# Sliding-window attention beside a squared-ReLU FFN: scores of later blocks in four 64x64 quarters, with a raw exp tile, other load and split orders, and wide dummy matmuls

## The chip, the cores and the metric

One core of a Trainium2 chip runs the whole program. The metric is the device time of one execution in microseconds (us); a figure for a kernel is the median of its runs. The profile is one further execution, recorded by the hardware profiler; its times count from the start of the first recorded instruction (the span).

## What is computed

The shapes are batch 8, heads 8, sequence 576, head width 64; the FFN has 4608 tokens (8 x 576), model width 512 and hidden width 2048. Results are float32.

```python
scores = scale * np.matmul(q, k.transpose(0, 1, 3, 2))
rel = pos[:, None] - pos[None, :]
bias = slopes[:, None, None] * (-np.abs(rel).astype(np.float32))[None, :, :]
mask = (rel >= 0) & (rel < window)            # window = 128
scores = np.where(mask, scores + bias[None], -1000000000.0)
attn = softmax(scores)                        # over keys
x = (attn @ v), heads side by side            # 4608 x 512
h = x @ w_in;  r = np.maximum(h, 0.0);  g = r * r
out = g @ w_out
```

A query sees itself and the 127 keys before it. With blocks of 128 queries and keys, a query block needs its own key block (where the key is not after the query) and the one before it (where the key's place in its block is greater than the query's place in its own). In each of these two 128x128 squares one 64x64 quarter is empty: in the own square, keys 64 to 127 for queries 0 to 63; in the square of the earlier block, keys 0 to 63 for queries 64 to 127.

## The kernel before

**Blocks.** Each batch's 576 positions make five blocks (`NKB`), four of 128 and one of 64; block m is number m % 5 (kb) of batch m // 5, 40 in all. The last block of a batch and the first of the next are scored together as a pair, in one P tile.

**Stages of a block.** `load_block` loads k, q and v, cast to bf16, through POOL's queue (block 0's k and q through SP's, in float32). `turn` transposes k and q: on TensorE for the blocks in `KQ_PE` (with evacuations to kqT on ScalarE and VectorE), otherwise by a DMA from SP's queue. `layout` places the score parts in the P tile: for a full block the earlier keys at columns 128 to 255 of each head, the own keys at 0 to 127. `score` takes units of half a block (4 heads) and makes one burst on TensorE of two units at the start and three from block 5 on. For each of a unit's two head pairs c and for each part there are two matmuls, one for each half of the array's 64 rows (heads on partitions 0 to 63 and 64 to 127 of kqT), which write two PSUM banks. Then for each bank an exp on ScalarE (L536) writes P from PSUM, and a multiplication on VectorE (L543) applies the mask with its ALiBi decay, in place. `mix` multiplies P by V with a column of ones beside it (L564), takes reciprocals of the sums (L587), normalizes into x (L592), and transposes x into xT on TensorE for blocks in `X_PE` (L610), otherwise by a DMA from SP's queue (L602).

**FFN.** Tokens go in nine groups of 512. `fc_step` computes a hidden slice with w_in (L667: 4 matmuls per 128 hidden columns), ReLU on ScalarE (L676), the square on VectorE into g (L683). `t_part` multiplies g by w_out (L729: 16 matmuls per 128 tokens), followed by an evacuation and a store. The first two groups are cut into pieces of tokens (`SPLIT`), so that they can start before all of the group's x is there.

**What sets the order.** Every step is a `Task` with assumed costs per engine, a key (its due time; `where` gives it for attention, with `AHEAD` and `LEAD` moving it forward), dependences, and slots that it takes and frees. `Plan.order` runs through these with a list scheduler and fixes the order of each engine; the program is then written out in that order, and engines only wait for semaphores. All PSUM slots are one pool of eight banks, and a score burst takes two for each unit. The ring sizes are in `size`. `FIRST` writes out the order of the first loads (b a block, i a quarter of w_in, o a quarter of w_out). `warm` at the start and `filler` in planned idle times of TensorE issue matmuls on zeros: `WARM` of them at the start, and afterwards `FILL` of the planned idle time until `UNTIL`; before `COLD` the plan counts TensorE at half speed. `QUARTERS` is set in this kernel but not used.

## Time and profile before

| quantity | value |
|---|---|
| median of 14 runs | 311.47 us (310.77 to 313.35) |
| profiled execution, its own time | 312.18 us |
| span of the profile | 310.4 us |
| TensorE matmul busy | 304.5 us (98%) |
| ScalarE busy | 179.1 us (58%) |
| VectorE busy | 161.2 us (52%) |
| exp L536, 128x512 | 124 instructions, 609 ns mean |
| mask L543, 128x512, single blocks | 96 instructions, 421 ns mean |
| score matmuls L507 | 576 |
| granted TensorE clock | 1.00 |

How to read the profile: busy time of TensorE overlaps from one matmul to the next, so differences between the starts of consecutive matmuls say what each costs in a stream. "PE" is TensorE's matmuls, "PEld" its weight loads, "DVE" VectorE, "ACT" ScalarE, "POOL" GpSimd, which here issues the loads, and "SP" the engine that issues stores and transposing DMAs. A row of groups gives the line, the engine, the operation, the tiles written and read, their shape, the count, busy us and mean ns. A row of waits gives the engine and line that waited, for what, the us in total, the number of times and the longest. A row for a stretch gives its length and, for PE, PEld, DVE, ACT and POOL in this order, busy us and the number of instructions, then the granted clock, the DMA share and GB/s. Time between engines matters only where TensorE waits for it.

### The profile page before, as it was taken

Reading aid. Unit: us, or ns where it says so; the run is one execution under the profiler, and the core shown is the slowest. Engines: PE = TensorE matmul, PEld = TensorE weight load, DVE = VectorE, ACT = ScalarE, POOL = GpSimd, SP = SyncE. Lnnn points to the kernel's source line nnn. Section 1 sums busy time; section 2 is a strip of 40 time slices with the busy share of each in tenths; the row PEclk is TensorE's granted clock in tenths of the full one; section 3 lists DMA queues with packets and bytes.
Section 4 is the critical chain, followed back from the end, with each engine's and each line's share of the span. In section 5 each row is a group of like instructions: output and inputs, shape, how many; then the busy total and the mean of one; then the engine's idle time right before and its main releaser. Section 6 shows DMA issues by size and latency. Waiting matters only on the chain.

```text
span 310.4 us, 7396 instructions
## 1 busy us (share of the span) xinstructions
PE 304.5 (98%) x2945; PEld 177.6 (57%) x2945; DVE 161.2 (52%) x475; ACT 179.1 (58%) x336; POOL 107.4 (35%) x134
## 2 busy tenths in 40 slices
...
GB/s 130 174 189 181 183 173 123 129 148 133 137 150 153 143 156 154 130 155 165 214 103 207 143 225 201 123 127 186 76 88 84 54 59 34 36 35 34 34 97 74
DMA packets 168115, 39.88 MB, mean 128 GB/s; under 512 B 159440, under 2 KB 163792, under 8 KB 168080
## 3 DMA queue, kind: packets, MB, share of 16 engines
...
q8 instruction: 23, 0.38, 0.5%
q14 instruction: 12, 0.10, 0.1%
...
## 4 chain that ended last, share of the span: by engine, by line
PE 93%; DMA 3%; POOL 2%; DVE 1%; ACT 0%; issue 0%; POOLq 0%
PE A L667 41%; PE A L729 40%; PE A L564 5%; PE A L507 5%; DMA kq<-in_q_dram 3%; PE A L458 1%; POOL kq L388 1%; PE A L610 1%; POOL vt L388 1%; ACT kqT L407 0%; DVE kqT L405 0%; POOL w_in_sb L357 0%; POOL dist L274 0%; DVE xT L405 0%; DVE g L683 0%
## 5 line engine op out<-in xcount | busy, mean ns | idle before, releaser
L667 PE MATMUL A<-xT,w_in_sb 128*128 128x512 bf16 (+3 forms) x960 | 150.6, 294 | 0.0
L729 PE MATMUL A<-w_out_sb,g 128*128 128x512 bf16 (+2 forms) x592 | 147.8, 373 | 0.0
L676 ACT ACTIVATE rt<-A 128x512 bf16<-128x512 f32 (+1 forms) x146 | 85.4, 600 | 73.1 <-PE A L667 62.9
L683 DVE TENSOR_TENSOR g<-rt 128x512 bf16<-128x512 bf16 (+1 forms) x146 | 60.9, 418 | 84.6 <-ACT rt L676 83.7
L667 PEld LDWEIGHTS <-w_in_sb 128*128 128x128 bf16 x960 | 71.0, 98 | 47.6
L729 PEld LDWEIGHTS <-g 128*128 128x128 bf16 x592 | 54.6, 98 | 56.5
L536 ACT ACTIVATE P<-A 128x512 bf16<-128x512 f32 (+1 forms) x132 | 68.4, 595 | 18.3 <-PE A L507 18.3
L543 DVE TENSOR_TENSOR P<-P,masks 128x512 bf16<-128x512 bf16 (+1 forms) x104 | 42.3, 411 | 19.9 <-ACT P L536 16.3
L388 POOL DMA_DIRECT2D vt<-in_v_dram x40 | 33.9, 850 | 52.6 <-PE A L564 39.9
L388 POOL DMA_DIRECT2D kq<-in_k_dram x39 | 33.2, 852 | 35.3 <-DMA kqT<-kq 21.6
L388 POOL DMA_DIRECT2D kq<-in_q_dram x39 | 33.4, 856 | 13.2 <-DMA kq<-in_k_dram 4.9
L699 ACT ACTIVATE osb<-A 128x512 f32<-128x512 f32 (+1 forms) x36 | 21.7, 602 | 22.2 <-PE A L729 22.0
L564 PEld LDWEIGHTS <-P 128*128 128x128 bf16 x576 | 26.3, 98 | 12.7
L592 DVE TENSOR_TENSOR x<-A,rec 128x256 bf16<-128x256 f32 (+1 forms) x80 | 32.3, 415 | 0.6
L707 POOL DMA_DIRECT2D out_dram<-osb x3 | 1.7, 563 | 80.3 <-ACT osb L699 80.3
L564 PE MATMUL A<-vt,P 128*128 128x65 bf16 x576 | 29.2, 193 | 0.0
L507 PEld LDWEIGHTS <-kqT 64*128 64x128 bf16 x576 | 15.0, 94 | 8.4 <-issue 7.6
L587 DVE RECIPROCAL rec<-A 128x4 f32<-128x4 f32 (+1 forms) x80 | 13.6, 177 | 8.9 <-PE A L564 7.7
L507 PE MATMUL A<-kqT,kqT 64*128 64x128 bf16 (+1 forms) x256 | 16.8, 211 | 0.7 <-ACT kqT L407 0.3
L507 PE MATMUL A<-kqT 64*128 64x128 bf16 (+1 forms) x320 | 17.3, 211 | 0.0
L543 DVE TENSOR_TENSOR P<-P,pair_masks 128x512 bf16<-128x512 bf16 x28 | 11.6, 419 | 3.4 <-ACT P L536 2.6
L407 ACT ACTIVATE kqT<-A 128x512 bf16<-128x512 bf16 (+1 forms) x9 | 5.2, 580 | 8.7 <-DVE kqT L405 5.9
...
## 6 DMA issues: line engine op xcount, KB each, us to landing
...
```

Of the source, the lines that this page charges most:

```text
L388: nc.gpsimd.dma_start(o, src[b, :, kb * 128:kb * 128 + n, :].rearrange("h s d -> s h d"))
L507: nc.tensor.matmul(slots[ms[0], 2 * j + half].tile.rearrange("p (c x) -> p c x", c=2)[:, c % 2, at:at + w], kqT[sk_of[mk].idx][rows, c, :] ...
L536: nc.scalar.activation(Pv(i), view(slot.tile.rearrange("p (c x) -> p c x", c=2)), AF.Exp, bias=0.0, scale=scale)
L543: nc.vector.tensor_tensor(pt, pt, view(mk), op=ALU.mult)
L564: nc.tensor.matmul(bank(slot_v)[:, hi * (D + 1):(hi + 1) * (D + 1)], Pt[sP.idx][:, place(h)].rearrange("p t q -> p (t q)")[:, at_of[m, par ...
L587: nc.vector.reciprocal(srec.tile[0:n, :], pv[0:n, :, D])
L592: nc.vector.tensor_tensor(xt[sx.idx][0:n, hf * 256:(hf + 1) * 256].rearrange("p (h e) -> p h e", h=4), pv[0:n, :, 0:D], srec.tile[0:n, :]. ...
L667: nc.tensor.matmul(bank(slot)[:, fi * w:(fi + 1) * w], w_in_sb[:, cc, fc * 128:(fc + 1) * 128], xT[:, cc, g * 512 + lo:g * 512 + hi], star ...
L676: nc.scalar.activation(srt.tile[:, 0:cols], slot.tile[:, 0:cols], AF.Relu, bias=0.0, scale=1.0)
L683: nc.vector.tensor_tensor(sg.tile[:, fcs[0]:fcs[-1] + 1, lo:hi], r, r, op=ALU.mult)
L699: nc.scalar.activation(so.tile[:, lo:hi], slot.tile[:, lo:hi], AF.Copy)
L729: nc.tensor.matmul(bank(slot)[:, lo:hi], sg.tile[:, fc, t * 128:(t + 1) * 128], w_out_sb[:, fc, lo:hi], start=fc == 0, stop=fc == FCB - 1)
```

## The change

**Scores.** With `QUARTERS = 6`, every block from number 6 on that is neither paired nor the first of a batch (kb 1, 2 or 3) is scored in quarters. For each head pair c the two 128x128 parts become four pieces: own keys 0 to 63 with queries 0 to 127, own keys 64 to 127 with queries 64 to 127, earlier keys 64 to 127 with queries 0 to 127, earlier keys 0 to 63 with queries 0 to 63. Each is a matmul per row half, with a 64x64 stationary operand, writing partitions 0 to 63 or 64 to 127 of the bank: eight matmuls per head pair instead of four. The columns of the upper keys are moved left by 64, so a head has 192 packed columns on every partition.

**Exps and masks.** The exp of such a bank reads 2 x 192 columns and writes a tile of a new ring `raw` (2 tiles). Two multiplications on VectorE, one per key half, take it to its place in a tile of another new ring `Pq` (2 tiles), columns 0 to 191 for keys 0 to 63 and 64 to 255 for keys 64 to 127. The quarters that are never written are set to zero once, by four memsets at the start. P is taken by the first mask rather than by the burst. The P-times-V matmuls stay as they are; the first of each half waits for the masks of its half.

**Constants.** `FIRST` loads blocks 0 to 3 before w_in. The first group is split in two pieces of 256 tokens (before: four of 128), the second in three (before: four). `X_PE` gains blocks 6, 13 and 21, `KQ_PE` loses block 11. `AHEAD`, `LEAD` and `EARLY` shift due times; `SOON` and the plan's cost of an exp (50 ns more) change what the planner assumes. The kq ring has 8 tiles instead of 7.

**Dummies.** A dummy matmul now streams up to 512 columns of zeros (four times the same 128) instead of 128; `WARM` is 24 x 128 columns instead of 16, `FILL` 0.7 instead of 0.8, `COLD` 8.2 us instead of 5.

The shortcut in `Plan.order` (left out below) skips candidates that can't be the best, and the field `n` of a task is not read.

```diff
--- before.py
+++ after.py
...
@@ -210,20 +213,20 @@
     NG = NT // 512
     NBLK = B * NKB
 
-    FIRST = "b0 b1 i0 b2 i1 b3 i2 o0 b4 i3 b5 o1 b6 o2 b7 o3 b8 b9"
-    SPLIT = {0: [(0, 128), (128, 256), (256, 384), (384, 512)], 1: [(0, 192), (192, 320), (320, 448), (448, 512)]}
-    EARLY = -20
-    AHEAD = {10: -60, 1: 30, 4: 30, 9: -60, 5: 0, 0: 0, 12: 60, 11: 0, 2: 60, 8: 30, 7: 60, 6: 0, 3: 30, 24: -30, 14: -60, 18: 30, 25: 30, 23: 30, 16: -30, 13: 60, 21: 0, 19: 30, 17: 0, 22: 0}
-    LEAD = 20
-
-    KQ_PE = [0, 1, 2, 3, 4, 5, 6, 7, 8, 11]
-    X_PE = [0, 1, 2, 3, 4, 5, 7, 8, 12, 17]
-    WARM = 16
-    FILL, UNTIL = 0.8, 26e3
-    COLD = 5000
-    QUARTERS = 99
+    FIRST = "b0 b1 b2 b3 i0 i1 i2 b4 b5 o0 b6 o1 b7 o2 i3 o3 b8 b9"
+    SPLIT = {0: [(0, 256), (256, 512)], 1: [(0, 192), (192, 320), (320, 512)]}
+    EARLY = 0
+    AHEAD = {10: -30, 1: 30, 4: 90, 9: -60, 5: 30, 0: 0, 12: 60, 11: 0, 2: -60, 8: 0, 7: 90, 6: 0, 3: -30, 24: 0, 14: -30, 18: 30, 25: 30, 23: 30, 16: -30, 13: 30, 21: 0, 19: 30, 17: 0, 22: 0, 20: 60, 15: 30}
+    LEAD = 40
+
+    KQ_PE = [0, 1, 2, 3, 4, 5, 6, 7, 8]
+    X_PE = [0, 1, 2, 3, 4, 5, 6, 7, 8, 12, 13, 17, 21]
+    WARM = 24
+    FILL, UNTIL = 0.7, 26e3
+    COLD = 8200
+    QUARTERS = 6
     V0 = 1
-    SHARE, SOON = 3, 500
+    SHARE, SOON = 3, 1500
     LONG, UNITS = 5, 3
     W_IN = [0, 4, 8, 12, 16]
     PAIR_AFTER, PAIR_KEY = 1, -140
...
@@ -250,11 +253,12 @@
         return [const.tile(shape, BF16, name=f"{name}_{i}") for i in range(n)]
 
 
-    size = {"kq": 7, "v": 7, "kqT": 5, "P": 2, "x": 4}
+    size = {"kq": 8, "v": 7, "kqT": 5, "P": 2, "x": 4, "Pq": 2, "raw": 2}
     kq = ring("kq", size["kq"], [128, 2, d_model])
     vt = ring("vt", size["v"], [128, H, D + 1])
     kqT = ring("kqT", size["kqT"], [128, 2 * C, 128])
-    Pt = ring("P", size["P"], [128, H, 2, 128])
+    Pt = {nm: ring(nm, size[nm], [128, H, 2, 128]) for nm in ("P", "Pq")}
+    raw = ring("raw", size["raw"], [128, H, 192])
     xt = ring("x", size["x"], [128, d_model])
 
     plan = Plan({"rec": 4, "rt": 3, "g": 2, "osb": OSB, **size}, BANKS, COLD, (SHARE, SOON))
...
@@ -338,11 +342,16 @@
     zero_first("v", vt, lambda t: t[64:128, :, 0:D], 512)
     zero_first("kq", kq, lambda t: t[64:128], 512)
     zero_first("kqT", kqT, lambda t: t[:, 0:C, 64:128], 128)
+    t_zero_P = []
+    for t in Pt["Pq"]:
+        t_zero_P.append(zero_task(t[0:64, :, 1, 64:128], 512))
+        t_zero_P.append(zero_task(t[64:128, :, 0, 0:64], 512))
+
     def warm():
-        for i in range(WARM):
-            nc.tensor.matmul(bank(sw)[:, 0:128], zero, zero, start=True, stop=True)
+        idle(bank(sw), WARM)
     sw = Slot("A")
-    plan.add({"PE": 53.5 * WARM}, -9.1e5, warm, [t_ones], [sw], [sw]).cols = 128 * WARM
+    tw = plan.add({"PE": 53.5 * WARM}, -9.1e5, warm, [t_ones], [sw], [sw])
+    tw.cols, tw.n = 128 * WARM, -(-WARM // 4)
 
     def load(key, ns, emit, deps=(), acq=()):
         return plan.add({"POOL": 900.0}, key, emit, deps, acq, dma=ns)
...
@@ -472,8 +481,9 @@
 
 
     def layout(ms):
-        sP = Slot("P")
         pair = len(ms) == 2
+        quarters = not pair and ms[0] % NKB and blk[ms[0] % NKB] == 128 and ms[0] >= QUARTERS
+        sP = Slot("Pq" if quarters else "P")
         work_of = []
         for i, m in enumerate(ms):
             b, kb, n, _, first = where(m)
@@ -500,7 +510,18 @@
             for sl in slots.values():
                 bank(sl)
             for (ms, sP, work_of, _), j in units:
-                for c in (2 * j, 2 * j + 1):
+                for c in (2 * j, 2 * j + 1) if sP.tag == "Pq" else ():
+                    m = ms[0]
+                    for part, k0, q0, q1 in ((1, 0, 0, 128), (1, 64, 64, 128), (0, 64, 0, 128), (0, 0, 0, 64)):
+                        mk = m - 1 + part
+                        lo = (c % 2) * 256 + at_of[m, part] + q0 - k0
+                        for half in range(2):
+                            rows = slice(half * 64, half * 64 + 64)
+                            nc.tensor.matmul(
+                                slots[m, 2 * j + half].tile[k0:k0 + 64, lo:lo + q1 - q0],
+                                kqT[sk_of[mk].idx][rows, c, k0:k0 + 64], kqT[sk_of[m].idx][rows, C + c, q0:q1],
+                                start=True, stop=True)
+                for c in () if sP.tag == "Pq" else (2 * j, 2 * j + 1):
                     for m, mk, w, at, _ in work_of:
                         for half in range(2):
                             rows = slice(half * 64, half * 64 + 64)
@@ -508,10 +529,13 @@
                                 slots[ms[0], 2 * j + half].tile.rearrange("p (c x) -> p c x", c=2)[:, c % 2, at:at + w],
                                 kqT[sk_of[mk].idx][rows, c, :], kqT[sk_of[m].idx][rows, C + c, 0:w],
                                 start=True, stop=True)
-        tm = plan.add({"PE": 220.0 + 2 * sum(max(w[2], 64) / 2.4 + 4 for u in units for w in u[0][2])}, due - 28, burst,
+        cost = 220.0 + 2 * sum(88.0 if u[0][1].tag == "Pq" else sum(max(w[2], 64) / 2.4 + 4 for w in u[0][2])
+                               for u in units)
+        tm = plan.add({"PE": cost}, due - 28, burst,
                       [t for u in units for w in u[0][2] for x in w[:2] for t in t_kq_of[x]] + chain["s"],
-                      [*slots.values()] + [u[0][1] for u in first_of],
+                      [*slots.values()] + [u[0][1] for u in first_of if u[0][1].tag == "P"],
                       [x for u in units if u[1] == 1 for w in u[0][2] for x in w[4]])
+        tm.n = 4 * sum(4 if u[0][1].tag == "Pq" else len(u[0][2]) for u in units)
         plan.bursts.append(tm)
         chain["s"] = [tm]
         for (ms, sP, work_of, due), j in units:
@@ -526,16 +550,37 @@
                     return t
                 return t.rearrange("p c (t q) -> p c t q", t=2)[:, :, lo:hi, 0:n]
 
-            for i in (2 * j, 2 * j + 1):
+            for i in (2 * j, 2 * j + 1) if sP.tag == "Pq" else ():
                 slot = slots[ms[0], i]
+                if i == 0:
+                    raw_of[ms[0]] = Slot("raw")
+                sr = raw_of[ms[0]]
+
+                def expo(i=i, slot=slot, sr=sr):
+                    nc.scalar.activation(raw[sr.idx][:, 2 * i:2 * i + 2],
+                                         slot.tile.rearrange("p (c x) -> p c x", c=2)[:, :, 0:192],
+                                         AF.Exp, bias=0.0, scale=scale)
+                te = plan.add({"ACT": act(384) + 50.0}, due - 28 + 3 * i, expo, [tm], [sr] if i == 0 else [], [slot])
+                for k0 in (0, 64):
+                    def mask(i=i, k0=k0, sr=sr, sP=sP):
+                        nc.vector.tensor_tensor(
+                            Pt["Pq"][sP.idx].rearrange("p h t q -> p h (t q)")[k0:k0 + 64, 2 * i:2 * i + 2, k0:k0 + 192],
+                            raw[sr.idx][k0:k0 + 64, 2 * i:2 * i + 2],
+                            masks.rearrange("p h t q -> p h (t q)")[k0:k0 + 64, 2 * i:2 * i + 2, k0:k0 + 192],
+                            op=ALU.mult)
+                    P_of[ms[0]][1].append(plan.add(
+                        {"DVE": dve(384, 2)}, due - 28 + 3 * i, mask, [te] + t_zero_P + t_mask,
+                        [sP] if i == 0 and k0 == 0 else [], [sr] if i == 3 and k0 else []))
+            for i in () if sP.tag == "Pq" else (2 * j, 2 * j + 1):
+                slot = slots[ms[0], i]
 
                 def Pv(i=i, sP=sP, view=view):
-                    return view(Pt[sP.idx][:, 2 * i:2 * i + 2].rearrange("p h t q -> p h (t q)"))
+                    return view(Pt["P"][sP.idx][:, 2 * i:2 * i + 2].rearrange("p h t q -> p h (t q)"))
 
                 def expo(i=i, Pv=Pv, view=view, slot=slot):
                     nc.scalar.activation(Pv(i), view(slot.tile.rearrange("p (c x) -> p c x", c=2)),
                                          AF.Exp, bias=0.0, scale=scale)
-                te = plan.add({"ACT": act(cols)}, due - 28 + 3 * i, expo, [tm], [], [slot])
+                te = plan.add({"ACT": act(cols) + 50.0}, due - 28 + 3 * i, expo, [tm], [], [slot])
 
                 def mask(i=i, pair=pair, Pv=Pv, view=view):
                     pt = Pv(i)
@@ -563,7 +608,7 @@
                     def emit(h=h, hi=hi, part=part, mk=mk, slot_v=slot_v):
                         nc.tensor.matmul(
                             bank(slot_v)[:, hi * (D + 1):(hi + 1) * (D + 1)],
-                            Pt[sP.idx][:, place(h)].rearrange("p t q -> p (t q)")[
+                            Pt[sP.tag][sP.idx][:, place(h)].rearrange("p t q -> p (t q)")[
                                 :, at_of[m, part]:at_of[m, part] + 128],
                             vt[s_in[mk, "v"].idx][:, h, :],
                             start=part == p0, stop=part == 1)
...
@@ -575,8 +620,8 @@
                             rel.append(sP)
                     new = hi == 0 and part == p0
                     last = plan.add({"PE": mm(D + 1)}, due - 12 + 4 * hf, emit,
-                                    [last, t_P[place(h) // 2], t_in[mk, "v"]]
-                                    + (t_P[2 * hf:2 * hf + 2] + chain["pv"] if new else []),
+                                    [last, t_in[mk, "v"]]
+                                    + (t_P[len(t_P) // 2 * hf:len(t_P) // 2 * (hf + 1)] + chain["pv"] if new else []),
                                     ([slot_v] + ([sx] if hf == 0 else [])) if new else [], rel)
             chain["pv"] = [last]
             srec = Slot("rec")
...
@@ -763,15 +809,18 @@
             t_part(g, u // 4, u % 4, key)
             key += 4
 
+    def idle(tile_, n):
+        for i in range(0, n, 4):
+            w = min(4, n - i)
+            nc.tensor.matmul(tile_[:, 0:128 * w].rearrange("p (w x) -> p w x", w=w), zero,
+                             zero.unsqueeze(1).to_broadcast([128, w, 128]), start=True, stop=True)
+
     def filler(slot, n):
         def emit():
-            for i in range(n):
-                if slot.turns:
-                    nc.tensor.transpose(bank(slot)[:, 0:128], zero, ident)
-                else:
-                    nc.tensor.matmul(bank(slot)[:, 0:128], zero, zero, start=True, stop=True)
-        t = Task({"PE": 107.0 * n / 2}, 0, emit, [t_ones] + [t_ident16] * slot.turns, [slot])
-        t.eng, t.start, t.end, t.seq, t.cols = "PE", 0.0, 0.0, 0, 128 * n
+            bank(slot)
+            idle(banks[slot.tag][slot.idx], n)
+        t = Task({"PE": 53.5 * n}, 0, emit, [t_ones], [slot])
+        t.eng, t.start, t.end, t.seq, t.cols, t.n = "PE", 0.0, 0.0, 0, 128 * n, -(-n // 4)
         return t
 
     def fill(tasks):
```

## Prediction

> **What bounds the kernel now.** I first read the busy shares and the chain that ended last, on the page.
>
> ```profile
> PE 304.5 (98%) x2945; PEld 177.6 (57%) x2945; DVE 161.2 (52%) x475; ACT 179.1 (58%) x336; POOL 107.4 (35%) x134
> ...
> PE 93%; DMA 3%; POOL 2%; DVE 1%; ACT 0%; issue 0%; POOLq 0%
> PE A L667 41%; PE A L729 40%; PE A L564 5%; PE A L507 5%; DMA kq<-in_q_dram 3%; PE A L458 1%; POOL kq L388 1%; PE A L610 1%; POOL vt L388 1%; ACT kqT L407 0%; DVE kqT L405 0%; POOL w_in_sb L357 0%; POOL dist L274 0%; DVE xT L405 0%; DVE g L683 0%
> ```
>
> The end is set by TensorE from start to finish. Busy time says little there, because matmuls overlap (a 512-column one lasts 379 ns, but the next starts 216 ns after it). So I take start-to-start times from the trace, which add up without overlap: the two FFN products (L667, L729) 252.0 us, probabilities times V (L564) 18.0, scores (L507) 17.1, transposes (L458, L440, L610) 7.9, dummy matmuls (L343, L770, L772) 11.3; sum 306.3. The first matmul starts at 1.0 us and 3.1 us follow the start of the last, which gives the span of 310.4. Only work in this list, and waits put into it, can move the time.
>
> Next, who TensorE waits for, and where the dummies lie (the four stretches are start-up, filling, attention beside FFN, FFN alone; the second answer counts the dummies only).
>
> ```profile
> PE A L458 <- DMA kq<-in_k_dram: 1.2, 1, 1.2
> PE A L343 <- DVE vt L322: 1.0, 1, 1.0
> PE A L507 <- ACT kqT L407: 0.3, 1, 0.3
> PE A L507 <- DVE kqT L405: 0.2, 1, 0.2
> ```
>
> ```profile
> 50.00:247.00 197.00, 197.00 (x1932) 108.33 (x1930) 117.37 (x345) 126.22 (x237) 71.07 (x86) 1.00 1.42 144
> ```
>
> ```profile
> 0.00:22.90 22.90, 11.40 (x121) 9.53 (x121) 0.11 (x1) 1.00 1.53 164
> ```
>
> All waiting lies in the first 23 us. From 50 to 247 us TensorE has no idle time and a full granted clock, VectorE is busy 117.4 of 197 us (60%) and ScalarE 126.2 (64%).
>
> **The score matmuls.** A quarter-packed block is any of kb 1 to 3 from block 6 on: 3 in each of 7 batches, 21 blocks, 84 head pairs. The cost of a head pair is read in the timeline of one burst.
>
> ```profile
> 103.63 0.38 PE L729 MATMUL A<-w_out_sb,g 128*128 128x512 bf16 x1
> 103.94 0.23 PE L507 MATMUL A<-kqT,kqT 64*128 64x128 bf16 x2
> 104.01 0.22 PE L507 MATMUL A<-kqT 64*128 64x128 bf16 x2
> 104.06 0.22 PE L507 MATMUL A<-kqT,kqT 64*128 64x128 bf16 x2
> 104.12 0.22 PE L507 MATMUL A<-kqT 64*128 64x128 bf16 x2
> ...
> 104.56 0.22 PE L507 MATMUL A<-kqT 64*128 64x128 bf16 x2
> 104.72 0.39 PE L667 MATMUL A<-xT,w_in_sb 128*128 128x512 bf16 x1
> ```
>
> Each "x2" is the two row halves of the array working side by side, 3 to 4 ns apart, and such a pair takes 56 ns: 53 for 128 columns plus the 3 ns step. A head pair has two of them, 112 ns. In the burst at 63.8 us, pairs with 64 columns start 25 to 29 ns apart although each brings two weight loads, so columns set the pace and an instruction costs next to nothing.
>
> The change makes eight 64x64 matmuls of this head pair: pairs A (128 columns, lower keys), B (64, upper), C (128, upper), D (64, lower). Nothing in this trace writes half of the output partitions, so the cost is bounded.
> *Low end:* upper and lower keys run side by side too. A and B start together; C follows B after 27 ns and ends at about 87; D follows A at 56 and ends at 83. The next head pair starts at about 86: 26 ns saved, times 84, is 2.2 us.
> *High end:* they take turns: 56+29+56+29 = 170 ns, 58 more, times 84, is 4.9 us lost.
> *Between:* weight loads. The Trainium skill speaks against the change here: "TensorEngine Tiling (Array Packing)", section Feature Incompatibilities, says that column tiling and Fast Weight Load exclude each other, and "TensorE: Matmul & The Clock Gate", section LDWEIGHTS, gives a plain load as columns / 1.2 ns, an estimate of 53 ns for 64 columns. The nearest rows are these.
>
> ```profile
> L440 PEld LDWEIGHTS A<-ident,kq 128*128 128x128 f32 x8 | 1.2, 185 | 0.0
> L458 PEld LDWEIGHTS <-kq 128*128 128x128 bf16 x72 | 4.4, 98 | 2.1 <-DMA kq<-in_k_dram 1.4 <-DMA kq<-in_q_dram 0.3
> ```
>
> A load of 4-byte weights lasts 87 ns longer than one of bf16, which fits slow loads of about that price. If the two key halves load side by side but slowly, C waits for its weights until 57 ns, D until 61, the next A until 114: 114 ns against 112, a loss of 0.2 us over 84. By the row of fast bf16 loads it is 86 ns.
> I take 86 ns, -2.2 us: a 64-column load is half the size of those now hidden inside 25 to 29 ns, and the four tiles use separate weights. The rule keeps a case of its own.
>
> Changing the array's split costs time: 312 ns from the start of the last 512-column matmul to the burst against 216, and as much on leaving (148 after the second of a pair against 53), 96 ns each way. Eight of the bursts from 50 us on hold units of both kinds (those with 64-column pair units among 128-column ones), so each gains one switch inside: 8 x 0.096 = +0.8 us; zero if the switch between two 64-row splits is free.
>
> **Exps and masks.** An exp goes from 512 to 384 columns: 84 x (609 - 500) = 9 us less on ScalarE (531 and 490 ns are the rows at 128x384). A mask of 421 ns becomes two on 64 partitions each; 64x256 and 128x256 normalizations take 408 and 416 ns, so half the partitions do not halve it, and the row at 384 columns is 348 ns: 168 x 348 - 84 x 421 = +23 us on VectorE. Both count nothing on the path as long as TensorE keeps FFN matmuls to run: VectorE goes to (117.4+23)/197 = 71%. A burst's masks take 12 x 348 = 4.2 us instead of 2.5; behind them on VectorE queue the squares of L683, which feed L729, and the reciprocals of L587. The new waits (an exp for its raw buffer, freed by the last mask two blocks earlier; a first mask for P) sit on ScalarE and VectorE, while the burst itself no longer waits for P. If this cover is gone, each of the 14 bursts with quarters would show up to 1.7 us. I take 0. Four memsets of 485 ns join VectorE's start-up (14.9 of 22.9 us busy): 0 to +0.5, taken 0.
>
> **Start-up.** Loads arrive in one queue in issue order. In the trace v of blocks 0 and 1 is in at 9.4 us, the first w_in quarter at 13.0, block 2 at 16.7, w_in 1 at 19.1, block 3 at 21.8, w_in 2 at 24.2. A block takes about 2.6 us, a weight quarter 2.4. The new order puts blocks 2 and 3 ahead: the first weights land at 9.4 + 5.2 + 2.4 = 17.0 if nothing stalls, at 24.2 - 4.8 = 19.4 if the same five items end when they do now. FFN starts later than today (16.2), but finds the x of four blocks, about 5.5 us of attention already done, and then 3.5 us of FFN for each weight quarter that takes 2.4 to land, so no gap follows. Unfilled time until then is 17.0 - 1 - 5.5 = 10.5 to 12.9 us; now it is 21.9 - 9.1 = 12.8 us until 22.9 (9.1 is the useful work in it). So -2.3 to +0.1, and up to +1 if block 3's x comes after its turn. I take -0.5, near the end with the same total. w_in 3 and w_out 3 come late in both orders (45.9 us now), with PV and the second group to cover them. WARM, FILL, COLD and wide dummies change only dummies in idle time, at the same columns; the clock is granted in full in all slices: 0, and up to +0.5 if a wide one sits in front of late data.
>
> Coarser splits: 64 x (4 x 55.9 - 2 x 109.2) ns for group 0 and 64 x 2.6 for group 1: -0.5 us. Blocks 6, 13 and 21 move the transpose of x to TensorE, 12 x 56 ns, block 11's eight of K and Q go to a DMA: +0.67 - 0.45 = +0.2. These moves take two transposes net from SP's queue, behind which stores wait; stores are not late before the end. The other loads on POOL wait for free buffers (39.9 us on L564), so one more kq buffer and the shifted due times are taken at 0.
>
> **Sum.** -2.2 + 0.8 - 0.5 - 0.5 + 0.2 = -2.2 us, so the profiled span goes from 310.4 to 308.2. The profiled execution took 312.18 us, 1.8 outside its span, and is 0.7 above the median of the runs, 311.47. I apply the difference to the median: 309.3 us.
>
> **Rivals.** *Slow weight loads*: 114 ns a head pair, +0.2 in place of -2.2: 311.7 us. For it: the rule and the 185 ns row. Against: half the columns per load.
> *Column halves take turns* (the slower end): 170 ns a head pair, 170 - 112 = 58 ns times 84 = +4.9, sum +4.9: 316.4 us. It decides as soon as a head pair takes more than 112 ns, since the rest sums to 0. For it: no instruction in this trace works beside another on the same rows. Against: the row halves overlap with a 3 ns step.
> *VectorE or the new start-up order becomes the wait*: 0.2 us in each of 14 bursts plus 1 us at the start, with slow loads or half their gain: about 313.5 us. For it: VectorE at 71% and in-order queues. Against: no wait of TensorE after 23 us today.
>
> **Chances.** Forecast case 0.50 (309.3, by itself 307 to 311), slow loads 0.25, taking turns 0.15, late masks or start-up 0.10. A measurement can tell about 0.3%, 0.9 us, from no change. Faster: 0.45 of the first, 0.07 of the second, 0.01 of the last: 0.53. Same: 0.05 + 0.10 + 0.02 = 0.17. Slower: 0.30. The range runs from 307.0 (the start-up at its best end) to 313.5, leaving out the taking of turns.
>
> **What would show it.** Right: the score group's start-to-start sum falls from 17.1 to near 15.7 us, head pairs of quarters start 80 to 90 ns apart, dummies and waits before 23 us stay within 1 us of 12.8, and TensorE still waits for nobody after that. Wrong: 170 ns head pairs, or any wait of TensorE for VectorE's masks, x or g between 50 and 247 us.

## The result, and the profile after

The changed kernel takes 315.15 us (median of 10 runs, 313.59 to 318.43) where the kernel before took 311.75 beside it (47 runs). The ratio is 1.0098, with a 95% interval of 1.008 to 1.0117: about 3.1 us slower. The forecast was 309.3, 2.2 us faster. The profiled execution took 314.26 us, 0.9 below the median of its runs; its span grew from 310.4 to 312.5 us. A few executions that disturbances lengthened are left out of the ratios.

Here are the busy shares and the chain that ended last, from the page of the kernel after. (L713 and L775 are now the two FFN products, L609 is P times V, L520 the quarters, L528 the other score matmuls, L467 and L449 the transposes of k and q, L655 that of x, L815 the dummies.)

```profile
PE 302.6 (97%) x2998; PEld 167.9 (54%) x2998; DVE 184.9 (59%) x566; ACT 171.0 (55%) x338; POOL 106.1 (34%) x132
...
PE 85%; DVE 4%; DMA 4%; POOL 3%; ACT 1%; issue 1%; POOLq 0%; ACTq 0%
PE A L775 38%; PE A L713 37%; PE A L609 5%; DMA w_in_sb<-in_moe_w_in_dram 4%; DVE Pq L566 3%; PE A L520 3%; POOL kq L397 2%; PE A L528 1%; POOL vt L397 1%; ACT raw L560 1%; PE A L655 1%; PE A L467 1%; POOL w_in_sb L366 0%; DVE x L637 0%; ACT kqT L416 0%
```

TensorE held 93% of the chain and now holds 85%. Two names are new in it, a load of w_in (4%) and the quarter masks of L566 (3%), while the scores went from 5% to 4% in all. The waits of TensorE name the same two.

```profile
PE A L713 <- DMA w_in_sb<-in_moe_w_in_dram: 2.2, 3, 1.3
PE A L467 <- DMA kq<-in_q_dram: 1.0, 2, 0.7
PE A L815 <- DVE vt L326: 1.0, 1, 1.0
PE A L815 <- ACT kqT L416: 0.6, 1, 0.6
PE A L609 <- DVE x L637: 0.6, 1, 0.6
PE A L609 <- DVE Pq L566: 0.5, 2, 0.3
PE A L449 <- DMA kq<-in_q_dram: 0.4, 1, 0.4
PE A L528 <- ACT kqT L416: 0.4, 1, 0.4
```

Before, no row stood for w_in, x or a mask. Start-to-start sums say where the span's 2.1 us came from. In them a wait counts with the matmul that stands before it:

| part of TensorE's time, us | before | after |
|---|---|---|
| two FFN products | 252.0 | 254.1 |
| P times V | 18.0 | 19.7 |
| scores | 17.1 | 16.9 |
| transposes | 7.9 | 10.3 |
| dummies | 11.3 | 7.3 |
| sum | 306.3 | 308.4 |

The FFN should have lost 0.5 us by its coarser pieces and gained 2.1. Behind FFN matmuls lie two of the three waits for w_in (0.50 and 1.49 us) and a wait for x at 112 us (0.79, shown below), where the kernel before has one wait of 0.4 us for kqT: -0.5 + 2.78 - 0.4 is about 1.9 of the 2.1. P times V holds 1.7 us more: the first wait for w_in (0.65) and three waits for quarter masks (0.43, 0.38 and 0.31). All waits above 40 ns in front of P times V after 40 us, wherever they count, sum to 2.3 us; before there is none. The transposes hold 0.2 us more work and 2.0 us of waits for q (1.4 of them idle time in the waits view). The dummies shrank by 4.0 us, which is idle time that waits took over. The scores hold a wait of 0.8 us for kqT at 14.0 us, so that their sum falls by only 0.2 although the bursts got shorter.

**The scores got cheaper.** One burst of three quarter units in the kernel after ("x4" is the four tiles of two matmul pairs):

```profile
51.03 0.24 PE L520 MATMUL A<-kqT 64*64 64x128 bf16 x4
51.09 0.22 PE L520 MATMUL A<-kqT,kqT 64*64 64x128 bf16 x4
51.14 0.22 PE L520 MATMUL A<-kqT 64*64 64x128 bf16 x4
51.18 0.22 PE L520 MATMUL A<-kqT,kqT 64*64 64x128 bf16 x4
51.23 0.22 PE L520 MATMUL A<-kqT 64*64 64x128 bf16 x4
51.26 0.22 PE L520 MATMUL A<-kqT,kqT 64*64 64x128 bf16 x4
...
51.53 0.22 PE L520 MATMUL A<-kqT,kqT 64*64 64x128 bf16 x4
51.68 0.75 PE L713 MATMUL A<-xT,w_in_sb 128*128 128x192 bf16 x7
```

Two of these rows make a head pair: 51.09 to 51.18 to 51.26, 88 ns each where 112 stood. Only the first head pair of a burst is some 20 ns longer. The burst falls from 776 to 652 ns. Mixed bursts grow: with one quarter unit and two pair units from 787 to 863 ns, with two and one from 781 to 810.

**The stretches.** From 50 to 247 us, and the dummies until 22.9:

```profile
50.00:247.00 197.00, 196.23 (x2134) 105.98 (x2132) 136.13 (x418) 115.14 (x232) 71.39 (x86) 1.00 1.45 142
```

```profile
0.00:22.90 22.90, 7.53 (x26) 2.62 (x26) 0.11 (x1) 1.00 1.59 159
```

TensorE was busy without a gap in the first of these before (197.00); it now stands for 0.8 us. VectorE is at 136.1 of 197 us (69%). The dummies fell from 121 instructions to 26. The clock stayed at 1.00.

**The start.** The wait for the third weight quarter, in TensorE's timeline of the kernel after (the bracket is the idle time before the row and what ended it):

```profile
17.89 1.27 PE L713 MATMUL A<-xT,w_in_sb 128*128 128x256 bf16 x10 [0.49 <-DMA w_in_sb<-in_moe_w_in_dram]
...
20.39 0.39 PE L713 MATMUL A<-xT,w_in_sb 128*128 128x256 bf16 x2 [0.34 <-DMA w_in_sb<-in_moe_w_in_dram]
...
21.52 0.39 PE L655 MATMUL A<-ident,x 128*128 128x128 bf16 x4
...
24.34 0.72 PE L713 MATMUL A<-xT,w_in_sb 128*128 128x256 bf16 x5 [1.33 <-DMA w_in_sb<-in_moe_w_in_dram]
24.90 0.61 PE L467 MATMUL A<-ident,kq 128*128 128x128 bf16 x8
25.35 0.39 PE L655 MATMUL A<-ident,x 128*128 128x128 bf16 x4
```

The quarters of w_in landed at 17.84, 20.34 and 24.30 us. The x of blocks 2 and 3 was transposed only at 21.5 and 25.35 us, so until then each weight quarter had one piece of 256 tokens to work on: 16 matmuls of 109 ns, 1.75 us, for loads that come 2.5 and 4.0 us apart.

**The masks.** The groups of the kernel after, then VectorE's timeline at a late mask, then TensorE's:

```profile
L566 DVE TENSOR_TENSOR Pq<-raw,masks 64x384 bf16<-64x384 bf16 x168 | 59.1, 352 | 9.6 <-ACT raw L560 6.3
...
L560 ACT ACTIVATE raw<-A 128x384 bf16<-128x384 f32 x84 | 35.7, 501 | 4.3 <-PE A L520 3.8
```

```profile
107.55 4.44 DVE L566 TENSOR_TENSOR Pq<-raw,masks 64x384 bf16<-64x384 bf16 x12 [0.45 <-ACT raw L560]
112.02 0.18 DVE L632 RECIPROCAL rec<-A 128x4 f32<-128x4 f32 x1
112.24 0.42 DVE L729 TENSOR_TENSOR g<-rt 128x512 bf16<-128x512 bf16 x1
112.58 0.42 DVE L637 TENSOR_TENSOR x<-A,rec 128x256 bf16<-128x256 f32 x1
```

```profile
112.04 0.39 PE L775 MATMUL A<-w_out_sb,g 128*128 128x512 bf16 x1
113.05 0.40 PE L609 MATMUL A<-vt,Pq 128*128 128x65 bf16 x8 [0.62 <-DVE x L637]
```

Twelve masks hold VectorE for 4.44 us. The reciprocal and the normalization queued behind them end at 113.0, and the P-times-V matmuls that stand next in TensorE's order (they need the slot that the normalization frees) begin then. The 0.62 us of idle time is 0.79 by starts.

### The profile page after: what moved, and what is told of

Its sections match the earlier page's. It is cut to its first block, busy times and chain, and to the rows that moved or that the text cites. A ratio compares the mean times of both kernels' runs of the same rounds, so it can differ in the third digit from the quotient of the medians.

```text
span 312.5 us, 7590 instructions
## 1 busy us (share of the span) xinstructions
PE 302.6 (97%) x2998; PEld 167.9 (54%) x2998; DVE 184.9 (59%) x566; ACT 171.0 (55%) x338; POOL 106.1 (34%) x132
## 4 chain that ended last, share of the span: by engine, by line
PE 85%; DVE 4%; DMA 4%; POOL 3%; ACT 1%; issue 1%; POOLq 0%; ACTq 0%
PE A L775 38%; PE A L713 37%; PE A L609 5%; DMA w_in_sb<-in_moe_w_in_dram 4%; DVE Pq L566 3%; PE A L520 3%; POOL kq L397 2%; PE A L528 1%; POOL vt L397 1%; ACT raw L560 1%; PE A L655 1%; PE A L467 1%; POOL w_in_sb L366 0%; DVE x L637 0%; ACT kqT L416 0%
## 5 line engine op out<-in xcount | busy, mean ns | idle before, releaser
L713 PE MATMUL A<-xT,w_in_sb 128*128 128x512 bf16 (+3 forms) x768 | 149.6, 326 | 2.2 <-DMA w_in_sb<-in_moe_w_in_dram 2.2
L775 PE MATMUL A<-w_out_sb,g 128*128 128x512 bf16 (+2 forms) x592 | 149.6, 374 | 0.0
L722 ACT ACTIVATE rt<-A 128x512 bf16<-128x512 f32 (+1 forms) x148 | 86.5, 591 | 98.7 <-PE A L713 80.2
L713 PEld LDWEIGHTS <-w_in_sb 128*128 128x128 bf16 x768 | 68.6, 98 | 53.6 <-DMA w_in_sb<-in_moe_w_in_dram 2.8
L775 PEld LDWEIGHTS <-g 128*128 128x128 bf16 x592 | 54.1, 98 | 54.2
L566 DVE TENSOR_TENSOR Pq<-raw,masks 64x384 bf16<-64x384 bf16 x168 | 59.1, 352 | 9.6 <-ACT raw L560 6.3
L560 ACT ACTIVATE raw<-A 128x384 bf16<-128x384 f32 x84 | 35.7, 501 | 4.3 <-PE A L520 3.8
L397 POOL DMA_DIRECT2D kq<-in_q_dram x39 | 33.5, 860 | 12.8 <-DMA vt<-in_v_dram 4.9
L581 ACT ACTIVATE P<-A 128x512 bf16<-128x512 f32 (+1 forms) x48 | 23.7, 577 | 3.6 <-PE A L528 3.5
L609 PEld LDWEIGHTS <-Pq 128*128 128x128 bf16 x336 | 15.6, 97 | 10.0 <-DVE Pq L566 1.2
L632 DVE RECIPROCAL rec<-A 128x4 f32<-128x4 f32 (+1 forms) x80 | 12.8, 173 | 12.3 <-PE A L609 11.3
L609 PE MATMUL A<-vt,Pq 128*128 128x65 bf16 x336 | 17.4, 193 | 1.2 <-DVE x L637 0.6
L609 PEld LDWEIGHTS <-P 128*128 128x128 bf16 x240 | 10.8, 98 | 4.8
L609 PE MATMUL A<-vt,P 128*128 128x65 bf16 x240 | 11.8, 193 | 0.0
L520 PEld LDWEIGHTS <-kqT 64*64 64x64 bf16 x672 | 8.4, 108 | 6.0 <-issue 5.7
```

Of the source, the lines that this page charges most:

```text
L397: nc.gpsimd.dma_start(o, src[b, :, kb * 128:kb * 128 + n, :].rearrange("h s d -> s h d"))
L520: nc.tensor.matmul(slots[m, 2 * j + half].tile[k0:k0 + 64, lo:lo + q1 - q0], kqT[sk_of[mk].idx][rows, c, k0:k0 + 64], kqT[sk_of[m].idx][ro ...
L560: nc.scalar.activation(raw[sr.idx][:, 2 * i:2 * i + 2], slot.tile.rearrange("p (c x) -> p c x", c=2)[:, :, 0:192], AF.Exp, bias=0.0, scale ...
L566: nc.vector.tensor_tensor(Pt["Pq"][sP.idx].rearrange("p h t q -> p h (t q)")[k0:k0 + 64, 2 * i:2 * i + 2, k0:k0 + 192], raw[sr.idx][k0:k0 ...
L581: nc.scalar.activation(Pv(i), view(slot.tile.rearrange("p (c x) -> p c x", c=2)), AF.Exp, bias=0.0, scale=scale)
L609: nc.tensor.matmul(bank(slot_v)[:, hi * (D + 1):(hi + 1) * (D + 1)], Pt[sP.tag][sP.idx][:, place(h)].rearrange("p t q -> p (t q)")[:, at_o ...
```

## The experiments

After the result the theory was that two things cost time, the new order of the start (with w_in late) and the masks (late on VectorE), each between 1 and 2 us, against a score gain of 0.8. The rivals were that one of them is all of it, and that the quarter matmuls themselves cost what their own rows don't show. The expectations were written before each run and name the theories as they then stood. All ratios are to the kernel before, run beside them.

### The parts of the change, one at a time

**q_old**: all of the quarter code (matmuls, raw tile, split masks) with every constant, the dummies and the kq ring of before.

```diff
-    FIRST = "b0 b1 b2 b3 i0 i1 i2 b4 b5 o0 b6 o1 b7 o2 i3 o3 b8 b9"
-    SPLIT = {0: [(0, 256), (256, 512)], 1: [(0, 192), (192, 320), (320, 512)]}
+    FIRST = "b0 b1 i0 b2 i1 b3 i2 o0 b4 i3 b5 o1 b6 o2 b7 o3 b8 b9"
+    SPLIT = {0: [(0, 128), (128, 256), (256, 384), (384, 512)], 1: [(0, 192), (192, 320), (320, 448), (448, 512)]}
...
```

> The quarter scores, the raw tile and the two masks, with every constant, ring size (kq) and dummy of the kernel before. Theory 1 (the loss is the new start-up: load order, splits and due times; quarters gain on TensorE and lose part of it to late masks): scores lose 1.5 us in the stretch 50 to 247 us, waits for Pq give back 0.5 to 2, the start up to 50 us stays as before; time 310.5 to 312.5, ratio about 0.999. Theory 2 (the loss is the quarters: two masks per bank put the P-times-V matmuls behind VectorE): 314 to 315, with the start unchanged and 3 us more waits after 50 us.

Measured: 321.71 us, ratio 1.0315 (1.0288 to 1.0342), the slowest of all. The waits of TensorE in it:

```profile
PE A L775 <- issue: 3.2, 1, 3.2
PE A L467 <- DMA kq<-in_k_dram: 1.9, 1, 1.9
PE A L609 <- DVE Pq L566: 1.2, 3, 0.5
```

No theory had the first row: TensorE stood 3.2 us from 75.7 us on, with everything it waits for there ("issue"). Five FFN matmuls then ran at the usual 216 ns or a little more, and from 80.4 us on seven took 427 ns each: the granted clock is 0.5 for 3.4 us from 80.2 us. Nor had any the second, a wait for block 2's k in front of other work at 12.5 us. Masks were late as expected.

**new_const**: all constants, the ring and the dummies of after, no quarters.

```diff
-    QUARTERS = 6
+    QUARTERS = 99
```

> Every constant, the kq ring and the wide dummies of the changed kernel, but no block in quarters (and no memsets of Pq). Theory 1: FFN work done by 50 us is about 3 us behind the kernel before, no waits in the middle; time 313.5 to 314.5, ratio about 1.008. Theory 2: as before within 0.3%, 311 to 312.5.

Measured: 313.5 us, 1.0051 (1.0031 to 1.007). The constants alone cost 1.6 us, half of the whole loss. The late P times V is gone: as in the kernel before, no wait above 40 ns stands in front of one after 40 us.

**q_inplace**: the kernel before, with the quarter matmuls writing their usual columns; exps and masks as before.

```diff
+                for c in (2 * j, 2 * j + 1) if quarters else ():
+                    for part, k0, q0, q1 in ((1, 0, 0, 128), (1, 64, 64, 128), (0, 64, 0, 128), (0, 0, 0, 64)):
...
+                        lo = (c % 2) * 256 + at_of[m, part] + q0
```

> The kernel before with nothing changed but the score matmuls: eight 64x64 matmuls per head pair from block 6 on, written to their usual columns; the exp still covers 512 columns, the mask 128x512 in place (the two empty quarters hold whatever the bank held, and the mask multiplies it by 0). Both theories: TensorE's scores 1.3 to 1.6 us shorter, VectorE and ScalarE as before. If theory 1's account of the masks holds, the time is 310.0 to 310.5, ratio 0.995 to 0.997. If the score gain is lost anyway to another wait (no masks in play), 311 to 312.

Measured: 315.76 us, 1.0121 (1.0096 to 1.0146), where a gain was expected. The scores are cheaper (16.3 us); the loss is one standstill, which TensorE's timeline shows in front of the last two of a run of 64-column matmuls:

```profile
75.69 1.97 PE L679 MATMUL A<-xT,w_in_sb 128*128 128x64 bf16 x62
80.96 0.23 PE L679 MATMUL A<-xT,w_in_sb 128*128 128x64 bf16 x2 [3.29 <-issue]
81.03 1.46 PE L741 MATMUL A<-w_out_sb,g 128*128 128x512 bf16 x6
```

**first_old**: the kernel after with the load order, pieces and `EARLY` of before.

```diff
-    EARLY = 0
+    EARLY = -20
...
```

> The changed kernel with load order, group splits and EARLY of the kernel before; the other constants stay new. If the late w_in quarters are the start-up's loss: waits for w_in at 17 to 24 us (2.7 us) go, time 312 to 313, ratio about 1.002 to 1.004. If due times and transposes (AHEAD, LEAD, KQ_PE, X_PE) are the loss: still 314.5 to 315.5.

Measured: 317.48 us, 1.0175 (1.0148 to 1.0201), 2.3 us slower than the kernel after. It too stands for "issue", 2.5 us up to 77.5 us in front of the last two of a run of 64-column matmuls; a late pair mask costs 1.2 us at 69.6, and k 1.4 us at 12.2. The standstill is as large as the difference, so the run suggests that fine pieces bring it, and says nothing sure of the load order.

### What stops TensorE with nothing to wait for

In q_inplace the standstill comes when TensorE has gone quickly through many instructions. A 64-column matmul and its weight load are two instructions in 29 ns; a quarter burst has 96 in 0.65 us. Its instructions arrive as 16 KB transfers on a queue of their own, at 62.34, 70.17 and 77.79 us in q_inplace. (The kernel before has 23 such transfers for 5890 matmuls and weight loads on TensorE, which is 256 for each.) Theory: TensorE ran out of code. Rivals: the row tiles of L520 themselves, or a wait that the profile doesn't record.

**inplace_coarse** gives q_inplace the pieces of the kernel after, hence fewer small matmuls.

```diff
-    SPLIT = {0: [(0, 128), (128, 256), (256, 384), (384, 512)], 1: [(0, 192), (192, 320), (320, 448), (448, 512)]}
+    SPLIT = {0: [(0, 256), (256, 512)], 1: [(0, 192), (192, 320), (320, 512)]}
```

> The kernel before with quarter score matmuls in their usual columns (as in q_inplace) and only the group splits of the changed kernel, which drop the 64-column pieces of group 1. Theory 3 (q_inplace lost to the loading of TensorE's code: 64-column matmuls and quarter bursts use up 256 instructions in less time than one 16 KB block takes to arrive, and TensorE stood for 3.3 us at 77 us with nothing to wait for): that standstill is gone, 311.0 to 312.3. If q_inplace lost because eight small matmuls disturb the order of the rest: still 315 to 316.

Measured: 314.55 us, 1.0081 (1.0058 to 1.0103). The standstill is gone, but coarse pieces of the first group with the old load order start late: the first output tile is evacuated at 51.8 us, 48.9 in q_inplace. Inconclusive as a time.

**inplace_g1** joins only the last two pieces of the second group.

```diff
-    SPLIT = {0: [(0, 128), (128, 256), (256, 384), (384, 512)], 1: [(0, 192), (192, 320), (320, 448), (448, 512)]}
+    SPLIT = {0: [(0, 128), (128, 256), (256, 384), (384, 512)], 1: [(0, 192), (192, 320), (320, 512)]}
```

> q_inplace (the kernel before with quarter score matmuls in their usual columns) with one more edit: the last two pieces of group 1, 128 and 64 tokens, are one of 192, so the stretch of 64-column matmuls at 75 us is gone and start-up is that of the kernel before. Theory 3 (TensorE ran out of loaded code there): the standstill of 3.3 us goes and the scores' gain of 0.8 us shows, 311.0 to 312.2, ratio 0.998 to 1.002. If something else made q_inplace slow: 314.5 to 316.

Measured: 311.58 us, 0.9985 (0.9968 to 1.0001), 4.2 us less than q_inplace. 64 matmuls of 64 columns and 64 of 128 became 64 of 192, the standstill went, and the quarter matmuls are all still there. This rules the tiles out as a cause by themselves. (The kernel before with this join alone wasn't run, so not all of 0.9985 is the quarters'.)

**before_fine** goes the other way: no quarters at all, but two more 64-column pieces.

```diff
-    SPLIT = {0: [(0, 128), (128, 256), (256, 384), (384, 512)], 1: [(0, 192), (192, 320), (320, 448), (448, 512)]}
+    SPLIT = {0: [(0, 128), (128, 256), (256, 384), (384, 512)], 1: [(0, 192), (192, 320), (320, 384), (384, 448), (448, 512)]}
```

> The kernel before, no quarters, with group 1's piece of 128 tokens at 320 cut in two of 64: 64 matmuls more, 0.2 us more of TensorE by columns, and three stretches of 64-column matmuls in a row at about 72 to 80 us. If TensorE's code can't be loaded as fast as such matmuls use it up: a standstill of 2 to 5 us with nothing to wait for, 314 to 318. If the standstill in q_inplace and q_old needs quarters: 311.5 to 312.3.

Measured: 315.9 us, 1.0131 (1.0111 to 1.0151). The standstill is back, without a quarter in the program:

```profile
74.53 0.67 PE L667 MATMUL A<-xT,w_in_sb 128*128 128x64 bf16 x17 [1.84 <-issue]
75.13 0.23 PE L507 MATMUL A<-kqT,kqT 64*128 64x128 bf16 x2
75.19 0.26 PE L507 MATMUL A<-kqT 64*128 64x128 bf16 x2
75.25 0.31 PE L507 MATMUL A<-kqT,kqT 64*128 64x128 bf16 x2
75.35 0.32 PE L507 MATMUL A<-kqT 64*128 64x128 bf16 x2
75.46 0.32 PE L507 MATMUL A<-kqT,kqT 64*128 64x128 bf16 x2
```

A code transfer begins at 72.15 us, just before TensorE stops.

The traces settle the rival of a hidden wait by a count. When TensorE stops in q_inplace it has started 1247 weight loads, each with its matmul; in q_old the long stop comes at 1247 and a short one (0.4 us) at 1119; in first_old they come at 1119 and, 0.5 us long, at 863; in before_fine at 1119. These numbers differ by multiples of 128 loads and 128 matmuls, 256 instructions, as much as one code transfer holds, though other work stands at each place. A wait for data would not keep to such a grid.

The Trainium skill, "Runtime: NRT & Kernel Launch", section Instruction fetch mechanics, has the same 16 KB blocks of 256 instructions and says that fetching them is mostly hidden. By the page q_inplace and inplace_g1 should differ by little more than the 0.17 us that 64 matmuls more of fixed cost make (64 x 2.6 ns); they differ by 4.2. The measurement decides: in these stretches of short instructions the fetch was not hidden. What isn't shown: in q_inplace the block from 77.79 has landed at 78.9, and TensorE starts 2.0 us later; the trace doesn't say what happens in between.

In before_fine the clock falls after the gap. The score pairs in the rows above first take 60 ns, and from the third on 107, where 56 is usual:

```profile
75.20:78.60 3.40, 3.18 (x36) 2.10 (x38) 1.65 (x4) 2.47 (x6) 1.55 (x3) 0.51 2.04 153
```

This isn't the rule: after the longer gaps of q_inplace and first_old (3.3 and 2.5 us) 512-column matmuls start 216 ns apart at once, at a granted clock of 1.00. What decides it isn't shown.

### The start and its dummies

**nc_first**: new_const with the load order of before.

```diff
-    FIRST = "b0 b1 b2 b3 i0 i1 i2 b4 b5 o0 b6 o1 b7 o2 i3 o3 b8 b9"
+    FIRST = "b0 b1 i0 b2 i1 b3 i2 o0 b4 i3 b5 o1 b6 o2 b7 o3 b8 b9"
```

> new_const (no quarters) with the load order of the kernel before; the coarse splits and due times stay new. If the load order costs the 1.6 us of new_const: 311.2 to 312.2. If due times, transposes and dummies do: 313 to 314. If the order fits only the finer splits (256 tokens need block 1 before w_in helps): over 314.

Measured: 313.44 us, 1.0053 (1.0034 to 1.0072), the same as new_const. In place of waits for w_in there is one of 2.04 us for k at 11.8 us.

**inplace_new**: new_const with the in-place quarters of q_inplace.

> All constants and wide dummies of the changed kernel, quarter score matmuls in their usual columns with the old exp and mask (no raw tile, no Pq). If the masks are what quarters lose on the new constants: new_const (313.5) less 1.2 to 1.5, 312.0 to 312.4. If the quarters' instructions are: 314.5 to 315.5, as the changed kernel.

Measured: 313.91 us, 1.0053 (1.0035 to 1.0071), the same as new_const (1.0051). The quarters' gain of 0.8 us, 0.26%, isn't seen here; the two intervals can hide about that much. Against the kernel after (1.0098) this says that all that lies between them, the raw tile, the split masks and their memsets, costs about 1.4 us.

Then three kernels each add one part of the new constants to the kernel before: **order_only** takes `FIRST`, `SPLIT` and `EARLY`; **dummies_only** the wide dummies with `WARM`, `FILL` and `COLD`; **due_only** the due times, `SOON`, the blocks transposed on TensorE, the eighth kq tile and the costlier exp of the plan.

```diff
-    FIRST = "b0 b1 i0 b2 i1 b3 i2 o0 b4 i3 b5 o1 b6 o2 b7 o3 b8 b9"
+    FIRST = "b0 b1 b2 b3 i0 i1 i2 b4 b5 o0 b6 o1 b7 o2 i3 o3 b8 b9"
...
```

> The kernel before with only the load order, the group splits and EARLY of the changed kernel. If the order with its fitting splits is what new_const lost: 313 to 314. If due times or dummies are: 311 to 312 (the coarser pieces alone should give 0.5 us).

```diff
-    COLD = 5000
+    COLD = 8200
...
+            idle(banks[slot.tag][slot.idx], n)
```

> The kernel before with only the dummies of the changed kernel: wide matmuls, WARM 24, FILL 0.7, COLD 8.2 us (which also makes the plan count TensorE at half speed for longer). Predicted at 0 to +0.5 us: 311.5 to 312.2. If dummies in fewer, longer pieces delay the first attention blocks or let the clock fall: 313 or more.

```diff
-    SHARE, SOON = 3, 500
+    SHARE, SOON = 3, 1500
...
```

> The kernel before with only the due times, the choice of transposes (AHEAD, LEAD, KQ_PE, X_PE), SOON, the eighth kq buffer and the plan's 50 ns more per exp. If these are the cost of new_const: 313 to 314; otherwise 311.3 to 312.2 (two transposes more on TensorE, +0.2).

Measured: order_only 312.89 us, 1.0033 (1.0018 to 1.0048), with 1.8 us of waits for w_in; dummies_only 315.65 us, 1.0104 (1.0067 to 1.014); due_only 313.82 us, 1.0065 (1.0045 to 1.0085), with 1.1 us of waits for k. By their ratios these are +1.0, +3.2 and +2.0 us singly; together, in new_const, +1.6. The parts of the start don't add up. In dummies_only a wait of 2.0 us for k stands at 11.9 us with x and FFN work behind it, and then the clock falls (the 0.66 in the second row of its stretches); later, at 62.7 and 85.0 us, it waits 1.4 us in all for DMAs that transpose k and q:

```profile
10.00:15.00 5.00, 2.22 (x23) 1.11 (x20) 2.50 (x9) 1.49 (x4) 3.67 (x5) 1.00 1.80 174
15.00:20.00 5.00, 4.32 (x45) 2.89 (x46) 2.73 (x10) 2.66 (x5) 2.27 (x4) 0.66 1.85 182
```

**after_old_dummies**: the kernel after with the dummies of before.

```diff
-    WARM = 24
-    FILL, UNTIL = 0.7, 26e3
-    COLD = 8200
+    WARM = 16
+    FILL, UNTIL = 0.8, 26e3
+    COLD = 5000
...
```

> The changed kernel with the dummies of the kernel before (narrow, WARM 16, FILL 0.8, COLD 5 us). If the thin dummies cost in it what they cost alone (a start at a lower clock): 312.5 to 314. If they only cost with the old load order: 314.5 to 315.7.

Measured: 313.63 us, 1.0067 (1.0041 to 1.0092). By the ratios that is 0.31% or 1.0 us less than the kernel after, about as much as the two intervals can hide. Until 22.9 us its dummies take 10.0 us and its waits and other time beyond columns 1.7, together 11.7, where the kernel after has 7.3 and 4.7, 12.0; and no wait for w_in is left in it, also not the one of 1.49 us that begins at 22.75 us in the kernel after. So the order that the plan makes with `COLD` at 5 us meets the weights better. The waits for masks and x are still there.

### The masks

**mask_cost**: the kernel after, but the plan counts a quarter mask at the 352 ns that it takes. `dve(384, 2)` gives 272.

```diff
-                        {"DVE": dve(384, 2)}, due - 28 + 3 * i, mask, [te] + t_zero_P + t_mask,
+                        {"DVE": 352.0}, due - 28 + 3 * i, mask, [te] + t_zero_P + t_mask,
```

> The changed kernel with one number altered: the planner's cost of a mask on 64 partitions is 352 ns, as measured, instead of 272. Theory 2 in its narrow form (twelve masks in a row hold VectorE for 4.4 us where the plan has 3.3, so P-times-V and transposes of x are put on TensorE too early): the waits for Pq and x after 40 us (2.3 us) shrink below 0.7, time 312.8 to 313.6. If VectorE is simply short of time, the waits move and the time stays at 314.5 to 315.5.

Measured: 313.77 us, 1.0051 (1.0029 to 1.0074), 1.4 less than the kernel after. No instruction is cheaper; the plan only places P times V and x later. In its waits of TensorE one for a mask is left where there were two, and none for x:

```profile
PE A L609 <- DVE Pq L566: 0.5, 1, 0.5
```

The profiled execution is a quick one, 311.95 us, so most executions may have more waits than it shows. The change in time is clear without it: the intervals of the two kernels don't meet.

**after_both** puts this and the old dummies together.

> The changed kernel with the two edits that helped it singly: the dummies of the kernel before (313.6) and the planner's mask cost of 352 ns (313.8). If the two losses are separate (start-up and late masks), they add: 312.0 to 312.8, ratio 1.001 to 1.003. If they are one and the same: 313.5 to 314.

Measured: 312.56 us, 1.0024 (0.9999 to 1.0049). The two corrections lower the kernel after by 0.47% and 0.31%, and together by 0.74%, which fits two losses rather than one seen twice. (Against after_old_dummies the further gain is clear of the intervals; against mask_cost, 0.27%, it isn't.) What is left is 0.24%, not told from nothing.

**q_old_fixed**: q_old with the second group's pieces joined and the plan's costs measured, to get the quarters of the change without the standstill and without late masks.

```diff
-    SPLIT = {0: [(0, 128), (128, 256), (256, 384), (384, 512)], 1: [(0, 192), (192, 320), (320, 448), (448, 512)]}
+    SPLIT = {0: [(0, 128), (128, 256), (256, 384), (384, 512)], 1: [(0, 192), (192, 320), (320, 512)]}
...
-                        {"DVE": dve(384, 2)}, due - 28 + 3 * i, mask, [te] + t_zero_P + t_mask,
+                        {"DVE": 352.0}, due - 28 + 3 * i, mask, [te] + t_zero_P + t_mask,
```

> q_old (quarters with raw tile and two masks, all constants of the kernel before: 321.7 us) with the two suspected costs taken away: the last pieces of group 1 joined into one of 192 tokens (code loading) and the planner's costs of a mask and an exp on 384 columns set to the measured 352 and 500 ns (late masks). If these two are all that quarters cost: 311 to 312.5. If the extra 23 us of masks on VectorE cost by themselves: 313 to 316.

Measured: 314.85 us, 1.009 (1.0063 to 1.0116); 6.9 us less than q_old, and still slow. No standstill; the start is late. TensorE's timeline:

```profile
11.73 0.87 PE L609 MATMUL A<-vt,P 128*128 128x65 bf16 x17
14.06 0.40 PE L467 MATMUL A<-ident,kq 128*128 128x128 bf16 x4 [1.47 <-DMA kq<-in_k_dram]
...
19.78 0.55 PE L713 MATMUL A<-xT,w_in_sb 128*128 128x128 bf16 x7
```

The transposes of block 2 stand ahead of block 1's work, the granted clock is 0.5 for 3.4 us from 15.2 us on, and the first FFN matmul comes at 19.78 us, 16.23 before. The only thing new at the start is the four memsets on VectorE, so I held them for the cause.

**q_late_zero** moves these memsets behind the masks of the pairs; the order of the start is then that of the kernel before.

```diff
+                    for t in t_zero_P:
+                        t.deps += t_pair
```

> q_old_fixed (314.85 us) with one edit: the four memsets of Pq wait for the pair masks, so they leave the first 13 us alone and TensorE's order at the start is again that of the kernel before, matmul by matmul. If q_old_fixed lost its 3 us only because the memsets turned the planned order (block 2's transposes before block 1's ready work, a wait of 1.6 us for k, first FFN matmul at 19.8 instead of 16.2 us): 311.0 to 312.2. If 23 us more of masks on VectorE cost by themselves: 313 to 315.

Measured: 314.48 us, 1.0076 (1.0049 to 1.0103). A miss. With the old order, the k of block 2 itself landed later, at 16.20 us (15.22 before):

```profile
16.25 0.40 PE L467 MATMUL A<-ident,kq 128*128 128x128 bf16 x4 [2.98 <-DMA kq<-in_k_dram]
```

So the memsets are not, or not alone, the cause. Here too the clock is 0.5 for 3.4 us afterwards, from 17.9 us on, which by itself can cost up to half of that. Why loads land later in a program whose start has the same order stays open, and so does what it costs: inplace_g1 waits 2.6 us for this k in its profile, keeps the full clock, and isn't slow. In the middle q_late_zero still has a wait of 0.5 us for x and a stop of 0.4 us at 1119 weight loads.

### The best version

**inplace_all**: inplace_g1, with the paired units from block 6 on also as 64x64 matmuls that leave out the empty half of the 64-position block; one split of the array then holds through every later burst.

```diff
+                for c in (2 * j, 2 * j + 1) if both else ():
+                    for x, part, k0, q0, q1 in ((m, 0, 0, 0, 64), (m, 0, 64, 0, 64), (m, 1, 0, 0, 64),
+                                                (m + 1, 1, 64, 64, 128), (m + 1, 1, 0, 0, 128)):
```

> inplace_g1 with the pair units in 64x64 matmuls as well (64, 64 and 128 columns on the lower keys, 64 and 64 on the upper; the upper keys of a 64-position block, which are padding and masked to 0, are left out), so that no burst changes the array's split inside. Expected: the eight mixed bursts lose 123 ns each, 1.0 us, and 311.6 becomes 310.6, ratio 0.995 to 0.997. If the pair units get slower by their ten matmuls instead of six: as inplace_g1 or above.

Measured: 310.7 us, 0.9966 (0.9954 to 0.9978), faster than both kernels by more than the intervals. (The joined pieces of inplace_g1 are in it, so not all of the 0.34% is the quarters'.) The mixed bursts go from 863 to about 770 ns and from 810 to about 708 (some matmul records are missing from these). Exps and masks are those of before:

```profile
span 307.9 us, 8095 instructions
...
PE 298.3 (97%) x3271; PEld 175.4 (57%) x3313; DVE 161.3 (52%) x477; ACT 179.5 (58%) x338; POOL 107.6 (35%) x134
```

VectorE is back at 161 us. ScalarE spends again the 9 us that the packed columns saved, at no cost to TensorE. One caution: the exp here reads what an earlier matmul left in the empty quarter, and the mask's zero removes it only as long as that exp is finite.

## Why the prediction was wrong, step by step

**Score matmuls, taken at 86 ns a head pair: right.** It is 88, and the key halves do run side by side. This refutes both rivals on it: turns of the two halves (170 ns) and slow weight loads (114). The rule of the Trainium skill that I weighed, "TensorEngine Tiling (Array Packing)", section Feature Incompatibilities, says that column tiling excludes fast loads; if it does, the loads still hide in 88 ns, so no run here shows a price of it.

**Switches inside mixed bursts, +0.8: too small.** A pure burst saves 124 ns: six head pairs at 24 ns are 144, and its first head pair takes some 20 ns longer than the others. In the two kinds of mixed burst a quarter unit saves 2 x 24 = 48 ns, yet they grow by 76 and 30 ns: a switch costs 76 + 48 = 124 and 30 + 96 = 126 ns, the slower first head pair included, not 96. The scores then gain 10 x 124 - 4 x 76 - 4 x 30 = 816 ns: 0.8 us, where the sum had 1.4.

**"Both count nothing on the path" (masks): the step that failed in the middle.** The sizes were right, 501 and 352 ns against 500 and 348, and VectorE's 23.7 us more against 23. The condition that I wrote beside them, "as long as TensorE keeps FFN matmuls to run", is true of an engine that can choose. TensorE follows a written order, made with masks of 272 ns; behind 12 masks of 352 the order is 1 us ahead of VectorE, and it stands although FFN work is ready. I had the 4.2 us of masks in a row, and I named the reciprocals behind them; I never compared the plan's figure with the row. mask_cost prices this at 1.4 us, as much as inplace_new shows for raw tile, split masks and memsets together. My own sign of being wrong, a wait of TensorE for masks or x between 50 and 247 us, is what the waits show.

**Start-up, -0.5: wrong in sign, the step that failed at the start.** "3.5 us of FFN for each weight quarter" is the work of 512 tokens. The x of blocks 2 and 3 wasn't there, so each quarter had 1.75 us, less than a landing takes. Start-up and splits, which are what order_only has, I had at -1.0 together; it measured +1.0. My test, dummies and waits until 22.9 us near 12.8, even holds (about 12.0), but by luck: the longest wait begins at 22.75 and lies outside it. The landings were within my bounds at first (17.84), but the third took 4.0 us, not 2.4. The fourth quarter of w_in, which I called late in both orders, landed at 30.6 us before and 42.3 after; TensorE didn't wait for it.

**Dummies, 0 to +0.5: probably too little.** They were priced as filling of idle time alone, but `COLD` and the wide form go into the plan: after_old_dummies gives 1.0 us, at the edge of what its interval can tell, and dummies_only costs 3.2 on the kernel before. This overlaps with the start-up, as the w_in waits go with it. Memsets of 272 ns (I had 485) showed no cost of their own that a run could separate.

**Splits and transposes, -0.5 and +0.2: right by count**, 249.58 to 249.10 us for the columns and the fixed cost of the FFN matmuls, and 0.2 us for four transposes more. No run has them alone.

**Rivals.** The third, "VectorE or the new start-up order becomes the wait", at 313.5 us and a chance of 0.10, named what happened. It was short by 1.65 us, and my sum for it was wrong: 0.2 us in each of 14 bursts and 1 us at the start, with half the gain, make 314.7 us, and with slow loads 316.0; 313.5 comes out only with the full gain. So the upper end of my range contradicted my own terms. (The bursts with quarters are also 18, ten pure and eight mixed, not 14.) That 314.7 lies near the measured 315.15 is luck: it has 2.8 us for the masks, which cost 1.4. At 0.10 the rival was far too unlikely. "No wait of TensorE after 23 us today", which I set against it, says that the order of before fits its durations; it says nothing of a new order made with other ones.

**Not foreseen: code.** It doesn't show in the kernel after, which has 95 dummies and three pieces of tokens less (7590 instructions on all engines, q_old 8210, q_inplace 8068). It does stop q_old, q_inplace and first_old: with the fine pieces of before, a stop of 2.5 to 3.3 us is more than the 0.8 us that the quarters gain.

**Open.** The whole is in two parts: the constants alone cost 1.6 us (new_const), and raw tile, masks and memsets on top of them 1.4 us. The quarter matmuls between these two show no gain (inplace_new against new_const), where 0.8 us were due and the intervals can hide as much. Within the constants the parts don't add up when taken singly. With masks and dummies treated, after_both is still 0.24% or 0.7 us above the kernel before (0 to 1.5 by the interval), although scores, splits and transposes give back 0.8 + 0.5 - 0.2 = 1.1 us. Some 1.8 us are thus not placed one by one; the new order and due times are still in it, and its waits have 1.6 us for q and 0.5 for a mask. The later landings in q_late_zero have no cause shown. The new versions also spread more from run to run (mask_cost 311.5 to 316.0, the kernel before 311.0 to 313.2 beside it); I didn't find why.
